# Three tables rewritten: the order, the engines and the PSUM banks of a recorded program of 1187 operations

## The chip, the cores and the metric

The kernel runs on one core of one Trainium2 chip. A core has five instruction queues that run side by side: TensorE (PE, matrix products into PSUM), VectorE (DVE), ScalarE (ACT), GpSimd (POOL) and SyncE (SP), which here only starts DMA transfers. Each engine executes its queue in order. The metric is the device time of one execution in microseconds (us), taken over several runs; beside it stands one execution that was profiled, with the start and end of every instruction.

## The reference

The reference applies two layers, A and B, and then both once more to the result. S = 2048 positions, D = 512 channels, F = 1376, all in bf16:

```python
def A(q, k, v, shift_k, ssm_k, ssm_D):        # q is LayerNorm(x)
    k_shift = sum over t of k_pad[:, t:t+S] * shift_k[:, 3-t]      # 4 taps, along the positions
    kv = k_shift * v
    y = irfft(rfft(kv, 2*S) * rfft(ssm_k, 2*S))[:S]                # causal convolution, 2048 long
    return q * (y + kv * ssm_D)

def B(x, w1, b1, w2, b2):                     # x is LayerNorm(x)
    return gelu(layernorm(x) @ w1 + b1) @ w2 + b2

x = A_q
x = x + A(layernorm(x), k, v, ...);  x = x + B(layernorm(x), ...)
x = x + A(layernorm(x), k, v, ...);  x = x + B(layernorm(x), ...)
```

What A multiplies its q with, the convolution result y + kv * ssm_D, depends on k, v and the filters alone, so both applications share it.

## The kernel before, in words

**Recording and arranging.** The kernel function doesn't emit instructions. It calls `P.op(...)` for each operation, which records the engines that it may run on, what it reads and writes, its PSUM tile and a duration from the writer's own table. Then `arrange()` (line 214) gives each operation its place by three tables of the class `Prog`: `SEQ` is one sequence of all 1187 operation numbers, and an engine's queue is its own operations in that sequence; `ENGS` has a letter for each operation with a choice of engine (a for ACT, v for DVE, p for POOL); `BANKS` gives each PSUM tile its first bank of eight. Operations that follow each other in a bank get a dependence there. `sync()` derives from the queues which semaphore waits are needed, and `emit()` writes the five queues. Data dependences alone limit the order, and every wait is found anew from the tables.

**The convolution, done as a long transform in two matrix stages.** The halves of the time axis are handled one after the other (half 0 first, then half 1). The names are those of the code and of this text, with the lines where the instructions are issued:

- Warm-up: seven matmuls on zeros (L532), so that PE has work before data lands.
- taps: shift_k (4 taps x 512 channels) is transposed on PE (L541) and copied by DVE (L481); POOL makes four diagonal matrices of it (L548).
- ht0, ht1: the filter ssm_k is transposed on PE (L561), a half at a time, and copied out of PSUM by ACT (L480) or DVE (L481); POOL or DVE (L475) adds ssm_D at the first tap.
- h1, h2: the filter's transform. Stage 1 (h1, L578) and stage 2 (h2, L590) are matmuls against tables; each result goes through an evacuation from PSUM by ACT (L480) or DVE (L481).
- spread: half of stage 2's table S2 is built on the chip from a smaller table C, eight steps of 128 x 1024 by ACT (L519) or DVE (L520); the other half of S2 is loaded (tab_s, L470). A part of w1 is later loaded over C, so that load waits for the spread.
- fir0 to fir3 (first half of the positions): k is transposed on PE (L610) and copied, the 4-tap shift is done as matmuls against the diagonals (L635), and DVE multiplies by v (L641). fir4 to fir7 (second half) do the same by pairs (L663, product L672), with k transposed by DMA transposes on SP's queue (L800, "kt").
- x1, x2: the transform of kv, stages 1 and 2, through the same lines L578 and L590. The products of the two spectra are x2_0 and x2_1 on DVE (L475), where half-swapped copies of the filter's spectrum are made by DMAs on SP's queue (L460, ar<-ar). The "sums" (L475, 128x2048) add the two parts of the second half.
- i1, i2: the inverse transform, L695 and L717, again with evacuations by ACT or DVE.

**The two layers, by blocks.** The 16 slices of 128 positions go through A's last step and B in blocks, `BLOCKS` = ((1,1,2,2,2),(2,2,2,2)) slices for the two applications in the first half, and ((4,4),(4,4)) in the second. For each block: q (statistics of x on DVE, L831 and L832; then small steps L836, L838 and the negative mean, L843 on DVE or L846 on POOL; then the normalization, L856 on ACT or L857 on DVE), y (two products on DVE, L475), z (statistics again and a second normalization), a transpose of z (on PE, L908, for the first two blocks; by SP's DMA transpose, L900, for the rest), m1 (44 matmuls, L920, with gelu on ACT, L925) and m2 (matmuls L954, with the addition to x on DVE, L958; the very last slice in three pieces, L943 and L947).

While the blocks of the first half run, PE, DVE and ACT work on the second half's transform in between: h2_1, fir4 to fir7, x1_1, x2_1, the sums and i1_1.

**Loads.** All loads stand in SP's queue apart from three small ones on ACT's. SP executes its queue in order as well: a DMA that has to wait for an engine holds those behind it.

Of the kernel before, what the change touches and what calls it, by code (L numbers as in the profile page):

```python
# [36 lines left out]
class Prog:  # L37
# [7 lines left out]
        0, 46, 8, 45, 35, 2, 6, 3, 5, 36, 12, 9, 1, 10, 11, 25, 4, 44, 217, 7, 56, 197, 15, 50, 16, 57, 14, 13, 47,  # L45
        51, 58, 20, 52, 48, 73, 17, 24, 65, 74, 49, 137, 71, 66, 216, 43, 200, 59, 72, 138, 61, 23, 60, 101, 34, 99,
        102, 198, 62, 26, 63, 212, 30, 135, 37, 100, 38, 53, 390, 18, 39, 103, 22, 432, 27, 41, 105, 19, 104, 108,
        204, 42, 54, 28, 199, 106, 114, 21, 64, 55, 136, 116, 391, 40, 115, 69, 110, 392, 70, 393, 31, 67, 109, 107,
        111, 68, 394, 117, 33, 112, 395, 119, 29, 123, 118, 124, 143, 32, 144, 131, 120, 81, 113, 474, 213, 79, 82,
        125, 80, 126, 127, 132, 433, 434, 75, 128, 435, 76, 121, 133, 476, 122, 77, 304, 475, 78, 129, 134, 528, 91,  # L50
        130, 139, 92, 85, 140, 214, 94, 89, 86, 477, 175, 478, 93, 90, 215, 163, 176, 479, 205, 83, 584, 480, 164, 87,
        84, 145, 88, 187, 165, 171, 188, 96, 177, 167, 95, 172, 168, 149, 97, 296, 150, 146, 179, 98, 183, 170, 180,
        195, 191, 173, 210, 157, 192, 208, 174, 202, 169, 184, 201, 159, 189, 196, 161, 303, 160, 207, 181, 155, 211,
        185, 162, 203, 141, 193, 206, 142, 194, 224, 166, 158, 220, 190, 156, 186, 218, 178, 436, 221, 222, 182, 225,
        582, 230, 219, 223, 232, 481, 231, 228, 484, 530, 233, 226, 583, 229, 227, 151, 437, 147, 295, 152, 148, 234,
        153, 235, 284, 585, 529, 236, 291, 154, 396, 238, 397, 237, 531, 398, 242, 290, 239, 438, 399, 240, 439, 400,
        243, 485, 285, 401, 440, 244, 288, 241, 259, 402, 441, 403, 442, 532, 245, 443, 289, 404, 256, 405, 246, 444,
        533, 445, 424, 260, 209, 410, 422, 425, 586, 286, 446, 261, 423, 587, 406, 447, 294, 418, 257, 250, 407, 388,
        419, 414, 482, 411, 389, 448, 415, 258, 292, 456, 449, 466, 534, 457, 454, 483, 467, 412, 486, 455, 452, 588,
        293, 413, 458, 487, 408, 464, 409, 489, 420, 459, 468, 453, 488, 253, 287, 465, 490, 251, 469, 491, 416, 421,  # L60
        428, 492, 417, 252, 538, 297, 426, 493, 254, 450, 496, 247, 255, 429, 427, 497, 451, 248, 494, 460, 262, 249,
        461, 495, 265, 592, 539, 462, 266, 470, 589, 268, 267, 463, 430, 535, 270, 263, 471, 269, 536, 431, 472, 264,
        298, 537, 272, 540, 518, 541, 271, 504, 519, 543, 502, 505, 542, 590, 506, 503, 593, 512, 507, 544, 591, 510,
        545, 513, 594, 500, 546, 511, 299, 498, 501, 595, 516, 547, 499, 514, 473, 548, 508, 596, 301, 524, 549, 509,
        597, 550, 525, 300, 517, 551, 515, 598, 638, 305, 599, 600, 302, 520, 636, 601, 602, 277, 521, 604, 603, 637,
        312, 307, 313, 526, 639, 309, 605, 640, 522, 641, 306, 554, 308, 642, 273, 568, 646, 527, 552, 274, 569, 572,
        523, 275, 643, 562, 276, 556, 555, 560, 553, 564, 693, 561, 558, 557, 644, 566, 559, 647, 691, 570, 563, 624,
        571, 645, 610, 573, 278, 567, 606, 565, 612, 607, 692, 279, 574, 611, 613, 625, 324, 649, 310, 648, 316, 311,
        694, 280, 695, 575, 317, 283, 608, 696, 620, 609, 576, 621, 281, 325, 614, 697, 320, 577, 615, 322, 321, 282,
        314, 318, 701, 650, 578, 651, 315, 698, 579, 652, 699, 319, 653, 702, 654, 580, 700, 323, 703, 622, 655, 581,  # L70
        628, 623, 704, 656, 326, 706, 618, 657, 327, 705, 658, 338, 707, 746, 708, 334, 339, 709, 659, 328, 616, 626,
        619, 710, 354, 617, 747, 748, 335, 632, 340, 711, 633, 713, 336, 712, 350, 629, 627, 749, 351, 337, 714, 750,
        630, 330, 355, 329, 342, 751, 331, 634, 631, 672, 343, 332, 662, 752, 346, 673, 668, 387, 663, 356, 674, 669,
        385, 678, 347, 384, 670, 344, 386, 664, 675, 717, 665, 333, 719, 679, 660, 720, 666, 661, 341, 729, 671, 718,
        721, 345, 733, 722, 723, 730, 676, 352, 715, 677, 735, 724, 716, 727, 348, 667, 725, 734, 731, 353, 737, 732,
        753, 680, 349, 756, 686, 681, 357, 687, 736, 728, 726, 688, 635, 360, 860, 362, 361, 754, 689, 370, 857, 757,
        368, 371, 755, 758, 682, 759, 369, 761, 683, 363, 760, 762, 801, 372, 763, 764, 862, 358, 373, 803, 765, 364,
        359, 802, 366, 858, 804, 738, 768, 766, 805, 365, 806, 367, 684, 769, 807, 739, 859, 863, 864, 808, 376, 767,
        861, 865, 685, 378, 811, 866, 867, 809, 374, 690, 812, 379, 810, 741, 813, 868, 375, 814, 742, 377, 816, 869,
        782, 875, 774, 815, 872, 783, 772, 817, 876, 878, 818, 776, 873, 819, 870, 775, 770, 879, 773, 743, 820, 771,  # L80
# [914 lines left out]
```

## Time and profile before

| | |
|---|---|
| median of three runs | 236.95 us (236.30 to 237.21) |
| span of the profiled execution | 234.03 us |
| PE busy | 222.7 us, 95% |
| DVE busy | 178.7 us, 76% |
| ACT busy | 164.5 us, 70% |
| POOL busy | 55.5 us, 24% |
| granted TensorE clock | 1.00 throughout |
| DMA | 24.93 MB, mean 107 GB/s |

The span runs from the profiled execution's first instruction to its last. The median of the runs stands 2.92 us above it. An instruction counts as busy while it executes, which for matmuls is modelled; "idle before" is time in which an engine's next instruction waited, and the arrow names what ended that wait. A group of instructions that share a line, an engine, an operation and a shape is one row. The timelines join neighbouring instructions of the same kind, with their count, and give the start, the time that they took together and in brackets the wait ahead of the first.

In the names, ar is the one large SBUF buffer, sm the small one for statistics, ps PSUM, and in_..._dram and tab_... are inputs and tables in DRAM.

### The profile page before, as it was taken

What the parts mean: (1) busy time and instruction counts of PE and PEld (TensorE: products, weight loads), DVE (VectorE), ACT (ScalarE), POOL (GpSimd) and SP (SyncE); (2) the same over time, 40 slices, a digit from 0 to 9 for tenths busy, and PEclk for the clock granted to TensorE, in tenths of its full rate; (3) what the DMA queues carried; (4) which work ended last, traced back from release to release, by engine and by line L of the source; (5) the groups of instructions that cost most, each with busy time, mean ns of one, the idle gap of its engine ahead of it and who ended that gap; (6) DMA issues with size and microseconds to landing.
All of it is one profiled execution on the core that took longest, in us unless ns stands there. A gap on an engine that the chain in (4) does not pass through costs nothing.

```text
span 234.0 us, 6498 instructions
## 1 busy us (share of the span) xinstructions
PE 222.7 (95%) x2743; PEld 147.1 (63%) x2765; DVE 178.7 (76%) x362; ACT 164.5 (70%) x262; POOL 55.5 (24%) x113
## 2 busy tenths in 40 slices
PE   7989887999999999999999999999999999999995
PEld 3878776967868596677966576644444444444454
DVE  0699998999999999999999988781777569410222
ACT  2789999989968688999879986488058216802710
POOL 2270132006403405639303331204011120200000
PEclk9999999999999999999999999999999999999999
DMA  6999489928994360033500313401300130170202
GB/s 185 381 386 305 147 229 274 324 65 150 144 211 126 70 158 3 1 48 72 155 4 3 90 24 68 134 3 22 69 0 3 28 62 0 23 115 0 90 0 92
DMA packets 40106, 24.93 MB, mean 107 GB/s; under 512 B 23591, under 2 KB 33677, under 8 KB 40077
## 3 DMA queue, kind: packets, MB, share of 16 engines
q1 hardware_dynamic: 39778, 24.36, 39.7%
q8 instruction: 22, 0.36, 0.7%
q10 hardware_dynamic: 298, 0.16, 0.4%
q14 instruction: 8, 0.06, 0.1%
HBM read 13.23 MB, written 2.10 MB: 66 GB/s over the span
## 4 chain that ended last, share of the span: by engine, by line
PE 58%; DVE 24%; ACT 10%; issue 2%; POOL 2%; DMA 2%; SPq 0%; DVEq 0%
PE ps L920 23%; PE ps L954 23%; DVE ar L475 13%; ACT ar L480 9%; PE ps L695 4%; DVE sm L831 3%; PE ps L590 2%; DMA ar<-in_A_ssm_k_dram 2%; DVE ar L672 2%; DVE ar L958 2%; DVE ar L641 2%; PE ps L717 1%; POOL sm L836 1%; PE ps L578 1%; PE ps L635 1%
## 5 line engine op out<-in xcount | busy, mean ns | idle before, releaser
L925 ACT ACTIVATE ar<-ps,sm 128x256 bf16<-128x256 f32 (+5 forms) x143 | 65.7, 523 | 33.2 <-PE ps L920 32.9
L920 PE MATMUL ps<-ar 128*128 128x256 bf16 (+5 forms) x569 | 81.9, 297 | 0.4 <-ACT ar L480 0.2
L480 ACT ACTIVATE ar<-ps 128x1024 bf16<-128x1024 f32 (+3 forms) x77 | 71.1, 998 | 11.0 <-PE ps L578 3.4
L954 PE MATMUL ps<-ar 128*128 128x512 bf16 (+1 forms) x323 | 75.9, 379 | 1.5 <-issue 0.6
L920 PEld LDWEIGHTS ps<-ar 128*128 128x128 bf16 (+1 forms) x572 | 52.9, 100 | 27.5 <-ACT ar L480 1.1
L475 DVE TENSOR_TENSOR ar<-ar 128x512 bf16<-128x512 bf16 (+2 forms) x104 | 62.7, 646 | 1.5 <-ACT ar L480 0.8
L954 PEld LDWEIGHTS ps<-ar 128*128 128x128 bf16 (+1 forms) x341 | 32.4, 98 | 35.3 <-ACT ar L925 0.4
L958 DVE TENSOR_TENSOR ar<-ar,ps 128x512 bf16<-128x512 bf16 x31 | 20.8, 680 | 32.9 <-PE ps L954 32.9
L831 DVE BATCH_NORM_STATS2 sm<-ar 128x6 f32<-128x512 bf16 x64 | 42.5, 685 | 0.5
L856 ACT ACTIVATE ar<-ar,sm 128x512 bf16<-128x512 bf16 x39 | 30.6, 813 | 12.9 <-DVE sm L843 8.8
L836 POOL TENSOR_SCALAR sm<-sm 128x2 f32<-128x2 f32 (+2 forms) x22 | 9.9, 449 | 89.0 <-DVE sm L832 88.8
L838 POOL TENSOR_TENSOR sm<-sm 128x2 f32<-128x2 f32 (+2 forms) x26 | 21.7, 834 | 25.1 <-DVE sm L836 23.1
L590 PE MATMUL ps<-ar 128*128 128x64 bf16 x512 | 18.4, 193 | 1.5 <-DVE ar L481 0.7
L578 PE MATMUL ps<-ar 128*64 128x128 bf16 x512 | 17.9, 221 | 1.8 <-ACT ar L480 1.2
L590 PEld LDWEIGHTS ps<-ar 128*128 128x128 bf16 x512 | 16.8, 98 | 3.6 <-DVE ar L481 1.3
L578 PEld LDWEIGHTS ps<-ar 128*64 128x64 bf16 x512 | 14.9, 110 | 4.8 <-ACT ar L480 1.9
L481 DVE CAST ar<-ps 128x1024 bf16<-128x1024 f32 x12 | 14.6, 1218 | 1.2 <-PE ps L578 0.9
L846 POOL TENSOR_SCALAR sm<-sm 128x1 f32<-128x1 f32 x34 | 15.1, 460 | 1.6
L695 PE MATMUL ps<-ar 64*128 64x64 bf16 (+1 forms) x384 | 12.4, 203 | 1.0 <-DVE ar L475 0.9
L695 PEld LDWEIGHTS ps<-ar 64*128 64x128 bf16 (+1 forms) x384 | 11.8, 113 | 2.2 <-DVE ar L475 1.0
L857 DVE TENSOR_SCALAR ar<-ar,sm 128x512 bf16<-128x512 bf16 x25 | 10.3, 415 | 2.7 <-POOL sm L846 2.5
L788 DVE SCALAR_TENSOR_TENSOR ar<-ar,sm,ps 128x512 bf16<-128x512 bf16 x16 | 11.1, 740 | 0.3 <-PE ps L590 0.3
(45 smaller groups left out, 93.5 us busy)
## 6 DMA issues: line engine op xcount, KB each, us to landing
ar<-ar SPq DMA_DIRECT2D x16, 256.0 KB, 4.0
ar<-tab_s SPq DMA_DIRECT2D x9, 256.0 KB, 6.3
ar<-in_A_ssm_k_dram SPq DMA_DIRECT2D x8, 256.0 KB, 5.9
ar<-in_A_q_dram SPq DMA_DIRECT2D x8, 256.0 KB, 4.4
ar<-in_A_v_dram SPq DMA_DIRECT2D x8, 256.0 KB, 5.0
out_dram<-ar SPq DMA_DIRECT2D x7, 256.0 KB, 2.5
ar<-in_B_w_dram SPq DMA_DIRECT2D x4, 344.0 KB, 5.2
ar<-in_B_w_dram SPq DMA_DIRECT2D x5, 256.0 KB, 5.2
```

The costliest lines, as they stand in the source:

```text
L475: return P.op(eng, lambda e: e.tensor_tensor(o, a, b, op), dur, reads=[a, b] + list(more), writes=[o])
L480: return e.activation(dst, src(), AF.Copy)
L578: r = e.matmul(Q(tl, 64 * ri, 64, i * 128, [1, 128]), w, m, start=True, stop=True)
L590: r = e.matmul(Q(tl, 0, 128, i // 8 * 512 + i % 8 * 4, [32, 16], [1, 4]), w, m, start=True, stop=True)
L695: r = e.matmul(Q(tl, 0, 128, i, *([32, 16], [1, 4]) if split else ([1, 128],)), w, m, start=n == 0, stop=n == 1)
L831: P.op(DVE, lambda e, sj=sj, x=x: e.bn_stats(sj, x), 600.0, reads=[x], writes=[sj])
L838: P.op(POOL, lambda e: e.tensor_tensor(r, v, hf, ALU.pow), 420.0 + 149.0 * n, reads=[v, hf], writes=[r])
L856: return e.activation(o, x, AF.Identity, bias=u, scale=r)
L920: r = e.matmul(Q(tl, 0, rows, 0, [1, w]), a, m, start=dk == 0, stop=dk == 3)
L925: P.op(ACT, lambda e, dst=dst, tl=tl, rows=rows, bias=bias, w=w: e.activation(dst, Q(tl, 0, rows, 0, [1, w]), AF.Gelu_apprx_tanh, bias=bia ...
L954: r = e.matmul(Q(tl, 0, 128, 0, [1, 512]), ins[fc][0], ins[fc][1], start=fc == 0, stop=fc == 10)
L958: P.op(DVE, lambda e, x=x, tl=tl: e.tensor_tensor(x, x, Q(tl, 0, 128, 0, [1, 512]), ALU.add), 604.0, reads=[x], writes=[x], tile=tl)
```

## The change

Only the three tables are rewritten. No operation is added, removed or changed in what it reads, writes and computes. 46 operations change their engine (ACT has 263 operations instead of 266, DVE 364 instead of 362, POOL 92 instead of 91), 441 operations have another PSUM bank, and the sequence is another one throughout. The matmuls are the same.

```diff
 class Prog:
     SEQ = (
-        0, 46, 8, 45, 35, 2, 6, 3, 5, 36, 12, 9, 1, 10, 11, 25, 4, 44, 217, 7, 56, 197, 15, 50, 16, 57, 14, 13, 47,
-        51, 58, 20, 52, 48, 73, 17, 24, 65, 74, 49, 137, 71, 66, 216, 43, 200, 59, 72, 138, 61, 23, 60, 101, 34, 99,
...
+        8, 35, 0, 25, 36, 1, 37, 6, 5, 2, 9, 197, 11, 38, 3, 56, 57, 50, 10, 51, 12, 47, 48, 390, 432, 43, 58, 73, 4,
+        52, 74, 71, 65, 7, 391, 392, 66, 433, 13, 27, 49, 61, 72, 62, 31, 15, 59, 216, 45, 60, 101, 102, 99, 63, 100,
...
     ENGS = (
-            "pvavvvvvavpvpapapaaavaaaaavaavaavavvvppvvvaavvaaavaavvaaaaaaaaavaaaaavaaaavaaaaaaapppvaaaaaaaaaaaaaaaaaa"
...
+            "pvvavvvavvpapvpapaaavaaaaavaavaavavvappppaaavvaaavavvvaaaaaaaaavaaaaavaaaavaaaaaaappvpaaaaaaaaaaaaaaaaaa"
...
     BANKS = (
-            "26624320240260660466027405640260464422140204626240406006442460424046462022442640460444626002206020640220"
...
+            "20073220440262240466027610646260464026341344006200442066402460624023624022442660460444626004262606002224"
...
```

The rows below show the queues as the tables give them, one row for neighbouring instructions of the same kind, without times.

The first place is the head of the kernel, on ACT and DVE, as far as the filter's transposes and the first results of stage 1. 128x8x16x8 is a copy of ht0, 128x1024 an evacuation of a transform stage, 128x8x128 a copy of a transposed k, 128x64x16 a step of the spread. On ACT (a minus stands for the row before, a plus for the row now):

```order
 L470 DMA ar<-tab_small 128x464
+L460 DMA ar<-in_A_shift_k_dram 4x512
 L460 DMA ar<-in_A_ssm_D_dram 1x512
 L494 ACT_TABLE_LOAD
-L460 DMA ar<-in_A_shift_k_dram 4x512
-L480 ACTIVATE ar<-ps 128x8x16x8
+L480 ACTIVATE ar<-ps 128x8x16x8 x2
 L480 ACTIVATE ar<-ps 128x1024 x4
 L480 ACTIVATE ar<-ps 128x8x128
```

The shift_k load moved ahead of the ssm_D load, and a second ht0 copy stands at ACT's head. On DVE before:

```order
L481 COPY ar<-ps 128x8x16x8 x2
L481 CAST ar<-ps 128x1024
L481 COPY ar<-ps 128x8x128
L520 TENSOR_SCALAR ar<-ar,sm 128x64x16 x2
L481 COPY ar<-ps 128x4x4
L831 BN_STATS sm<-ar 128x6 x2
L481 COPY ar<-ps 128x8x128
L520 TENSOR_SCALAR ar<-ar,sm 128x64x16
```

And on DVE now:

```order
L481 COPY ar<-ps 128x4x4
L481 COPY ar<-ps 128x8x16x8
L831 BN_STATS sm<-ar 128x6 x2
L832 BN_AGGR sm<-sm 128x2
L836 TENSOR_SCALAR sm<-sm 128x1
L481 CAST ar<-ps 128x1024
L832 BN_AGGR sm<-sm 128x2
L520 TENSOR_SCALAR ar<-ar,sm 128x64x16 x2
```

The taps' copy (128x4x4) went to the head, one ht0 copy left, and two statistics of q stand ahead of the first cast. On PE the transposes of the taps moved in the same way, from behind h1_0's first matmuls to right behind the warm-up.

The second place is SP's queue where the tables of stage 2 (tab_s) and the second half of the filter (in_A_ssm_k_dram) are loaded. Before:

```order
L470 DMA ar<-tab_small 128x256
L460 DMA ar<-in_A_q_dram 128x1024
L460 DMA ar<-in_B_b_dram 128x10x1
L460 DMA ar<-in_A_ssm_k_dram 128x1024
L470 DMA ar<-tab_s 128x1024 x3
L460 DMA ar<-in_B_w_dram 128x1376
L460 DMA ar<-in_A_q_dram 128x1024
L470 DMA ar<-tab_s 128x1024
L460 DMA ar<-in_A_ssm_k_dram 128x1024
```

Now:

```order
L460 DMA ar<-in_A_ssm_k_dram 128x1024
L470 DMA ar<-tab_s 128x1024
L460 DMA ar<-in_B_w_dram 128x1376
L470 DMA ar<-tab_s 128x1024 x3
L460 DMA ar<-in_A_ssm_k_dram 128x1024
L470 DMA ar<-tab_s 128x1024 x3
L460 DMA ar<-in_A_ssm_k_dram 128x1024
```

The load of the part of w1 (128x1376), which waits for the spread's last reading of C, now stands ahead of eight loads of the tables and the filter instead of two. Farther ahead in the same queue, the first load of q went from the tenth place to the fifth, with k's other three loads and a table behind it; and the last of the eight DMA transposes of k (L800) went behind two transposes of z (L900) and four half-swaps (L460, 64x8x256).

The third place is DVE's queue around the long run of sums that i1_1 reads (128x32x64 is a sum or a product of x2_1, L958 the addition of m2). Before:

```order
L475 TENSOR_TENSOR ar<-ar 128x32x64 x2
L832 BN_AGGR sm<-sm 128x2
L475 TENSOR_TENSOR ar<-ar 128x32x64 x2
L958 TENSOR_TENSOR ar<-ar,ps 128x512
L475 TENSOR_TENSOR ar<-ar 128x32x64 x11
L958 TENSOR_TENSOR ar<-ar,ps 128x512
```

Now:

```order
L475 TENSOR_TENSOR ar<-ar 128x32x64 x3
L832 BN_AGGR sm<-sm 128x2
L475 TENSOR_TENSOR ar<-ar 128x32x64
L958 TENSOR_TENSOR ar<-ar,ps 128x512
L475 TENSOR_TENSOR ar<-ar 128x32x64 x12
L475 TENSOR_TENSOR ar<-ar 128x512
L958 TENSOR_TENSOR ar<-ar,ps 128x512
```

The run behind that L958 is of twelve instead of eleven, so one more sum stands behind the addition. Other additions of m2 stand farther forward in DVE's queue, the one of operation 635 at place 173 of DVE's operations instead of 190.

In the chain of z of the first block, the negative mean is computed on POOL (L846) instead of DVE (L843).

8 lines of the change are left out of this document (4 added, 4 removed), and 106 rows, old and new, of the table SEQ.

## The prediction

> **What bounds the kernel now.** I read the busy time by stretch first. The columns are the stretch's length, and then the busy time of PE, of its weight loads (PEld), of DVE, ACT and POOL, each with its instructions; then the granted clock, the DMA share and the rate.
>
> ```profile
> 5.70:41.30 35.60, 30.84 (x772) 27.05 (x770) 31.75 (x52) 32.70 (x35) 9.69 (x24) 1.00 0.89 285
> 41.30:56.40 15.10, 14.32 (x243) 11.87 (x244) 14.71 (x33) 13.89 (x18) 2.23 (x6) 1.00 0.69 181
> 56.40:121.40 65.00, 64.08 (x917) 48.19 (x927) 64.11 (x109) 57.05 (x114) 25.25 (x40) 1.00 0.44 95
> 121.40:227.30 105.90, 104.99 (x764) 55.10 (x775) 66.28 (x168) 59.58 (x97) 16.95 (x34) 1.00 0.18 41
> ```
>
> From 56.4 on PE is busy for all but 0.92 of 65.00 and all but 0.91 of 105.90 us, at the full clock. The diff changes no matmul, so little is to be had behind 56.4. Ahead of it PE idles 4.76 us of 35.60 and 0.78 of 15.10. What holds PE there is shown by the chain of work that ended last (start, duration, what):
>
> ```profile
> 34.14 1.85 ACT ar L480 x2
> ...
> 39.97 1.30 DVE ar L475 x2
> 41.27 0.05 issue
> 41.32 7.39 PE ps L695 x128
> 48.73 6.59 ACT ar L480 x8
> 55.37 0.41 PE ps L908 x4
> ...
> 56.46 0.84 PE ps L920 x12
> ```
>
> The inverse transform i1_0 (L695) begins at 41.32, when the last spectrum product x2_0 (L475 on DVE) is done; these products in turn read ACT's PSUM evacuations (L480). Then come evacuations of i1_0, the transposes of z0 (L908) and at 56.46 the first matmul of m1 (L920). By the two orders the same 55 PE operations stand ahead of i1_0 before and after, and the same 75 ahead of the first m1. So the forecast is: the shift of i1_0, plus the change of the chain to 56.46, plus what the later stretches lose or win.
>
> Next I asked for what ACT, DVE and POOL themselves waited in the first 42 us (total, times, longest):
>
> ```profile
> POOL ar L548 <- DVE ar L481: 3.1, 1, 3.1
> ACT ar L480 <- PE ps L561: 2.6, 1, 2.6
> ACT ar L480 <- PE ps L578: 2.3, 3, 1.4
> DVE ar L481 <- PE ps L561: 6.9, 2, 6.6
> ```
>
> And for ACT's own timeline (start, duration, idle ahead in brackets):
>
> ```profile
> 5.70 1.02 ACT L480 ACTIVATE ar<-ps 128x1024 bf16<-128x1024 bf16 x1 [2.63 <-PE ps L561]
> 8.14 4.69 ACT L480 ACTIVATE ar<-ps 128x1024 bf16<-128x1024 f32 x5 [1.42 <-PE ps L578]
> 16.41 1.94 ACT L480 ACTIVATE ar<-ps 128x1024 bf16<-128x1024 f32 x2 [0.73 <-PE ps L578]
> 18.23 1.15 ACT L519 ACTIVATE ar<-ar,sm 128x1024 bf16<-128x1024 bf16 x1
> 30.37 17.65 ACT L480 ACTIVATE ar<-ps 128x1024 bf16<-128x1024 f32 x19 [0.17 <-PE ps L590]
> ```
>
> From 5.70 on ACT is nearly full: 32.70 of 35.60, idle 2.90, half of it the gap of 1.42. DVE idles 35.60 - 31.75 = 3.85, of which 0.85 lies ahead of its first copy at 6.55 (the wait of 6.6 above); 3.00 remain. The last evacuation that x2_0 needs is the ninth of the run at 30.37 (17.65 / 19 = 0.93 each), so it ends at 38.73; four products stand behind it on DVE.
>
> **The change part by part.** All of it is order, engine and bank. The durations are:
>
> ```profile
> L480 ACT ACTIVATE ar<-ps 128x1024 bf16<-128x1024 f32 x27 | 25.6, 1033 | 2.9 <-PE ps L578 2.3 <-PE ps L590 0.6
> L481 DVE CAST ar<-ps 128x1024 bf16<-128x1024 f32 x8 | 9.8, 1220 | 0.9 <-PE ps L578 0.6 <-PE ps L590 0.3
> L480 ACT ACTIVATE ar<-ps 128x1024 bf16<-128x1024 bf16 x5 | 5.2, 1037 | 2.6 <-PE ps L561 2.6
> L481 DVE COPY ar<-ps 128x1024 bf16<-128x1024 bf16 x7 | 4.8, 683 | 7.6 <-PE ps L561 6.9 <-PE ps L610 0.7
> L856 ACT ACTIVATE ar<-ar,sm 128x512 bf16<-128x512 bf16 x1 | 0.8, 812 | 0.0
> L857 DVE TENSOR_SCALAR ar<-ar,sm 128x512 bf16<-128x512 bf16 x25 | 10.3, 415 | 2.7 <-POOL sm L846 2.5
> ```
>
> *ACT up to x2_0's last evacuation.* It takes four evacuations more (one of ht0, one transpose of fir3, one of x1_0, one of h1_1), gives up two (of ht0 and ht1) and one L856, and swaps two steps of the spread for two others: 4 x 1.035 - 2 x 1.037 - 0.81 = +1.26. Before, it worked 38.73 - 5.70 - 2.90 = 30.13 there; now 31.4. With all 2.90 of idle kept it ends at 40.0; with none, at 37.1. Two gaps have a reason to go. The ht0 copy that it takes is ready when the gap of 1.42 begins. And the taps (below) bring FIR work forward, behind which the gap of 0.73 stood. That leaves 0.75 idle and an end at 37.85. One product instead of four now follows the last evacuation, 0.65 by the chain (1.30 for two). So i1_0 begins between 38.5 and 40.7, that is 0.6 to 2.8 earlier, by ACT alone.
>
> *DVE up to the same point.* It gives up two bf16 copies and one cast (1.37 + 1.22), and takes two copies and one L857 (1.37 + 0.41): 0.8 less. With its 3.00 of idle kept and 0.5 lost at the head (next), it gains 0.3; with all idle gone, 3.8. Both engines have to be there. I take 1.7, the middle of ACT's range, since ACT is the fuller of the two.
>
> *Heads of the queues.* The taps' transposes go from behind h1_0 to right behind the warm-up matmuls, and the shift_k load ahead of ssm_D. POOL's diagonals (L548) waited 3.1 for the taps' copy, so FIR can begin about 1 us earlier: that is the 0.73 counted above. On DVE two BN_STATS of q now stand ahead of the first cast. They wait for a q load that moves from the tenth place of SP's load queue to the fifth; if it lands late, DVE stands with a cast behind it. From the start of a load to its landing:
>
> ```profile
> L460 SPq DMA_DIRECT2D ar<-in_A_k_dram x4: 432/432/435, 2.1 to 3.5; - x4
> ...
> DMA to landing us min/median/max: 5.5/5.8/6.1
> ```
>
> The fifth load is issued at about 2.6, so it lands at 8.1 to 8.7, where the first cast began at 8.59 before. Two BN_STATS then push that cast by 1.3, against one copy of 0.68 that DVE no longer does: from nothing to 0.6, taken as 0.5. The k loads behind it land a place later, half a microsecond; FIR reads them only after the taps: nothing, unless the taps are so early that k is then last.
>
> *z0's chain.* One mean step goes from DVE (L843) to POOL (L846), 0.27 for 0.14:
>
> ```profile
> 54.46 0.14 DVE L843 SCALAR_TENSOR_TENSOR sm<-sm 128x1 f32<-128x1 f32 x1
> 55.84 0.27 POOL L846 TENSOR_SCALAR sm<-sm 128x1 f32<-128x1 f32 x1
> ```
>
> That is 0.13; with the other engine's start I take +0.2, between 0 and the 1.3 of a rival below.
>
> *56.4 to the end.* The m2 additions (L958) stand earlier in DVE's queue, and DVE executes in order. What DVE waited for them over the whole run, the end of the spectrum sums, and what they feed:
>
> ```profile
> DVE ar L958 <- PE ps L954: 32.9, 12, 7.4
> ...
> 108.41 12.58 DVE L475 TENSOR_TENSOR ar<-ar 128x2048 bf16<-128x2048 bf16 x11
> ...
> 121.44 2.57 PE L695 MATMUL ps<-ar 64*128 64x64 bf16 x128
> ```
>
> The first matmul of i1_1 (121.44) needs all sixteen sums, done at 120.99: 0.45 spare. DVE's work ahead of the last sum falls by the 0.8 above and by one L857 (0.41), 1.2 in all; if its idle in the front falls with PE's, it keeps up with PE 1.7 earlier. I put zero here, with 0 to +3 as bounds. The sixth to eighth transposes of A_k and the FIR that reads them:
>
> ```profile
> L800 SPq DMA_TRANSPOSE ar<-in_A_k_dram x8: 1188/1268/2345, 49.3 to 61.2; - x8
> ...
> L663 PE MATMUL ps<-ar x176: 172/201/225, 69.4 to 78.0; 32*128 32x128 bf16 x80, 32*128 32x32 bf16 x32, 32*128 32x64 bf16 x32, 32*128 32x96 bf16 x32
> ```
>
> The eighth goes behind two transposes of z2 and four half-swaps, which wait for DVE; its FIR goes behind m1 of block 2, 5.7 us of PE work. I cost this at nothing; the FIR at 69.4 was covered by other matmuls, and without them the transpose would cost its own issue, 1.2 to 2.3. At the tail the order of matmuls and stores is nearly the same: nothing. The PSUM banks move for 441 operations; no wait for a bank stands out above, and I give them nothing.
>
> *Sum.* -1.7 + 0.2 = -1.5, on a profiled span of 234.03: 232.5. The median of the runs stands 2.9 above that span (236.95 - 234.03); with it 235.4.
>
> **The rivals.** *The front gains as worked out:* 235.4, with its own bounds. If all of ACT's 2.9 and the three products were saved it would be 3.4 (233.5); if only 0.6 at i1_0 and +0.2 at z0, 236.5.
>
> *DVE loses it in order (slower).* If the earlier L958 make DVE wait between 56 and 121, the sums come late and i1_1 with them. It can lose 0.45 (spare) + 1.2 (less work) + 0.9 (the front's idle, 1.7 - 0.8) = 2.55 before i1_1 is later than it was; from there the end is slower than before. One wait of the length that L958 showed elsewhere, 7.4, gives 4.85 on the end: 241.8; two thirds of such a wait, 4.9, give 2.35: 239.3. For it: DVE busy 64.11 of 65.00. Against: m2's matmuls are moved forward with their additions, and the window's whole idle time on DVE was 0.89.
>
> *Loads hold the front.* In SP's queue a w1 load now waits for the spread's last reading of the C table, and eight loads stand behind it, tables of h2_0 among them. The spread's last step on ACT ended at 19.4 (18.23 + 1.15). These loads were
>
> ```profile
> 16.96 3.36 SPq L470 DMA_DIRECT2D ar<-tab_s  x3
> ...
> 21.31 0.43 SPq L470 DMA_DIRECT2D ar<-tab_s  x1
> ```
>
> so the last table was issued at 21.3. Eight at 0.48 from 19.4 end at 23.2, 1.9 later, and land at 29. If h2_0 is ahead by then, it loses the 1.9: 237.3. Against: h2_0 reads half its table from the spread first.
>
> *POOL's steps are held beside DVE.* In z0's chain three steps run on POOL. A POOL step of 0.2 to 0.3 took this long beside three DVE products:
>
> ```profile
> 90.35 3.34 POOL L836 TENSOR_SCALAR sm<-sm 128x2 f32<-128x2 f32 x1 [8.07 <-DVE sm L832]
> ...
> 90.16 3.48 DVE L475 TENSOR_TENSOR ar<-ar 128x2048 bf16<-128x2048 bf16 x3
> ...
> L475 DVE TENSOR_TENSOR ar<-ar x104: 392/425/1237, 32.5 to 197.7; 128x512 bf16<-128x512 bf16 x64, 128x2048 bf16<-128x2048 bf16 x24, 128x1024 bf16<-128x1024 bf16 x16
> ```
>
> If each step waits out one product of 0.42, that is 1.3 in place of 0.2: 236.5. [...] Against it here: the step at 55.84 took its 0.27 while DVE was busy too.
>
> *Nothing on the path changes:* PE's idle in the front is put elsewhere, 236.95.
>
> **How the numbers follow.** A measurement of this kernel tells about 0.5% from no change, 1.2 us: faster is under 235.8, slower over 238.1. The front's gain 0.49; DVE's loss 0.26; late loads 0.13; POOL held 0.07; nothing 0.05. The last three lie within 0.5%. So faster 0.49, same 0.25, slower 0.26. The range goes from 233.5, the whole of ACT's idle gained, to 239.3, two thirds of a long L958 wait; beyond it lie half of DVE's rival (0.13) and little below.
>
> **What would show it.** In the changed kernel's profile i1_0 (L695) begins near 39.6 and the first L920 near 55; ACT has no gap of 1.4 at 6.7 to 8.1; L548 begins about 1 us earlier or more; DVE between 55 and 120 idles no more than 1 to 2 us; the first L695 of i1_1 stands near 120. The forecast is wrong if i1_0 stays behind 41, if a weight load of h2_0 names a DMA as what it waited for, or if L695 near 120 waits for DVE.

## The result

The changed kernel takes 238.97 us (median of four runs, 238.48 to 239.90) against 236.62 for the kernel before (four runs, 235.60 to 237.21): the ratio is estimated as 1.0119, with a 95% interval from 1.0081 to 1.0158. By the medians it is 2.35 us slower, a quotient of 1.0099; the ratios given below are estimates of the same kind, and need not be the quotients of the medians. The profiled spans say the same: 236.73 against 234.03.

The busy times by stretch, of the changed kernel (columns as in the prediction):

```profile
5.70:41.30 35.60, 30.87 (x783) 27.84 (x781) 31.15 (x49) 33.80 (x37) 10.99 (x28) 1.00 0.93 291
41.30:56.40 15.10, 14.26 (x244) 11.54 (x242) 14.75 (x32) 13.70 (x17) 4.03 (x13) 1.00 0.44 140
56.40:121.40 65.00, 61.49 (x903) 45.99 (x904) 60.59 (x105) 55.48 (x110) 20.19 (x35) 1.00 0.50 101
121.40:227.30 105.90, 105.90 (x780) 55.24 (x779) 70.20 (x176) 60.32 (x97) 16.97 (x35) 1.00 0.17 41
```

PE's idle time in the front is as it was (4.73 for 4.76). Between 56.4 and 121.4 it is 3.51 for 0.92: that is the loss. Behind 121.4 PE is full. The chain of work of the changed kernel, front part:

```profile
30.57 4.99 DMA ar<-ar
35.56 0.02 issue
35.58 0.87 DVE ar L475 x2
...
40.54 7.39 PE ps L695 x128
...
54.53 0.40 PE ps L908 x4
...
55.86 0.45 PE ps L920 x8
```

The front does gain: i1_0 begins at 40.54 for 41.32, the transposes of z0 at 54.53 for 55.37, m1 at about 0.7 earlier. But the chain goes through a DMA, a half-swap that lands at 35.56, where the prediction had ACT.

PE's own timeline shows where the middle lost it (idle ahead in brackets):

```profile
75.00 1.12 PE L663 MATMUL ps<-ar 32*128 32x128 bf16 x88 [0.83 <-ACT ar L856]
...
95.27 1.53 PE L578 MATMUL ps<-ar 128*64 128x128 bf16 x48 [1.05 <-ACT ar L925]
...
110.28 0.64 PE L590 MATMUL ps<-ar 128*128 128x64 bf16 x16 [1.54 <-ACT ar L480]
```

Measured from start to start, which leaves the modelled ends out, these cost 1.0, 1.2 and 1.7 us. Behind each stands another engine. POOL, then DVE, then ACT around the last two:

```profile
57.21 0.50 POOL L846 TENSOR_SCALAR sm<-sm 128x1 f32<-128x1 f32 x2
...
90.97 2.67 POOL L846 TENSOR_SCALAR sm<-sm 128x1 f32<-128x1 f32 x2
...
103.47 3.39 POOL L846 TENSOR_SCALAR sm<-sm 128x1 f32<-128x1 f32 x2
```

```profile
57.10 1.40 DVE L788 SCALAR_TENSOR_TENSOR ar<-ar,sm,ps 128x512 bf16<-128x512 bf16 x2
...
90.83 2.68 DVE L475 TENSOR_TENSOR ar<-ar 128x512 bf16<-128x512 bf16 x3
...
103.22 3.50 DVE L475 TENSOR_TENSOR ar<-ar 128x2048 bf16<-128x2048 bf16 x3
...
110.26 14.14 DVE L475 TENSOR_TENSOR ar<-ar 128x2048 bf16<-128x2048 bf16 x13 [1.68 <-ACT ar L480]
```

```profile
93.68 0.81 ACT L856 ACTIVATE ar<-ar,sm 128x512 bf16<-128x512 bf16 x1 [1.37 <-POOL sm L846]
...
106.89 1.52 ACT L856 ACTIVATE ar<-ar,sm 128x512 bf16<-128x512 bf16 x2 [1.72 <-POOL sm L846]
```

Such a pair of POOL steps takes 0.50 beside DVE's L788, which has one of its two large inputs in PSUM, and 2.67 and 3.39 beside DVE's products and sums L475, which have both in SBUF (the row at 90.83 is one product and two sums); it ends when they do (106.86 beside 106.72, 93.64 beside 93.51). No experiment takes the products and sums away from the step; that they hold it is read from these coincidences, and what in them does so is not shown. ACT's normalization L856 waits for it, the gelus and PSUM evacuations behind L856 wait in ACT's queue, and PE and then DVE itself wait for those. The trace of before has the steps of q6 (94.58) and of z6 (101.86) too, and the L856 that wait for them:

```profile
94.58 1.16 POOL L846 TENSOR_SCALAR sm<-sm 128x1 f32<-128x1 f32 x2
...
101.86 1.05 POOL L846 TENSOR_SCALAR sm<-sm 128x1 f32<-128x1 f32 x2
```

```profile
95.77 0.81 ACT L856 ACTIVATE ar<-ar,sm 128x512 bf16<-128x512 bf16 x1 [0.16 <-POOL sm L846]
...
103.68 1.57 ACT L856 ACTIVATE ar<-ar,sm 128x512 bf16<-128x512 bf16 x2
```

There q6's chain was held as well, one step earlier (3.34 at 90.35, in the prediction), and its mean was ready later than now, at 95.74 for 93.64. PE did not wait there: four evacuations of x1_1, with gelus among them, stood ahead of that L856 in ACT's queue. A pair of q7 took 4.54 at 108.54, and its L856 came at 118.25 only. The wait at 75 has a different cause, which the experiments show.

### The profile page after: what moved, and what is told of

The parts are those of the page before. It is cut to its first block, busy times and chain, and to the rows that moved or that the text cites. A ratio compares the mean times of both kernels' runs of the same rounds, so it can differ in the third digit from the quotient of the medians.

```text
span 236.7 us, 6529 instructions
## 1 busy us (share of the span) xinstructions
PE 224.0 (95%) x2765; PEld 146.7 (62%) x2765; DVE 179.7 (76%) x364; ACT 164.6 (70%) x259; POOL 53.2 (22%) x117
## 4 chain that ended last, share of the span: by engine, by line
PE 77%; DVE 7%; DMA 5%; ACT 4%; SPq 2%; POOL 2%; issue 1%
PE ps L920 32%; PE ps L954 29%; PE ps L695 5%; DMA ar<-in_A_k_dram 3%; DVE ar L475 3%; SPq L460 2%; ACT ar L480 2%; DMA ar<-ar 2%; PE ps L590 2%; PE ps L578 2%; DVE ar L481 2%; PE ps L635 2%; POOL sm L846 2%; DVE sm L831 2%; PE ps L717 1%
## 5 line engine op out<-in xcount | busy, mean ns | idle before, releaser
L925 ACT ACTIVATE ar<-ps,sm 128x256 bf16<-128x256 f32 (+5 forms) x143 | 66.4, 526 | 43.2 <-PE ps L920 42.9
L920 PE MATMUL ps<-ar 128*128 128x256 bf16 (+5 forms) x572 | 80.9, 297 | 0.0
L480 ACT ACTIVATE ar<-ps 128x1024 bf16<-128x1024 f32 (+3 forms) x79 | 72.3, 1002 | 8.9 <-PE ps L561 2.4
L954 PE MATMUL ps<-ar 128*128 128x512 bf16 (+1 forms) x341 | 78.3, 379 | 0.1
L475 DVE TENSOR_TENSOR ar<-ar 128x512 bf16<-128x512 bf16 (+2 forms) x104 | 63.2, 641 | 3.9 <-ACT ar L480 1.9
L958 DVE TENSOR_TENSOR ar<-ar,ps 128x512 bf16<-128x512 bf16 x31 | 21.0, 682 | 20.0 <-PE ps L954 19.7
L856 ACT ACTIVATE ar<-ar,sm 128x512 bf16<-128x512 bf16 x34 | 26.7, 808 | 7.4 <-POOL sm L846 5.0
L838 POOL TENSOR_TENSOR sm<-sm 128x2 f32<-128x2 f32 (+2 forms) x26 | 21.6, 830 | 44.7 <-DVE sm L836 43.0
L836 POOL TENSOR_SCALAR sm<-sm 128x2 f32<-128x2 f32 (+2 forms) x19 | 4.9, 257 | 86.8 <-DVE sm L832 85.7
L590 PE MATMUL ps<-ar 128*128 128x64 bf16 x512 | 18.4, 193 | 1.8 <-ACT ar L480 1.7
L578 PE MATMUL ps<-ar 128*64 128x128 bf16 x512 | 17.6, 221 | 2.4 <-ACT ar L480 1.3
L590 PEld LDWEIGHTS ps<-ar 128*128 128x128 bf16 x512 | 16.8, 98 | 3.7 <-ACT ar L480 2.5
L578 PEld LDWEIGHTS ps<-ar 128*64 128x64 bf16 x512 | 14.8, 110 | 4.8 <-ACT ar L480 2.3
L846 POOL TENSOR_SCALAR sm<-sm 128x1 f32<-128x1 f32 x39 | 15.3, 408 | 1.8
L857 DVE TENSOR_SCALAR ar<-ar,sm 128x512 bf16<-128x512 bf16 x30 | 11.7, 410 | 5.0 <-POOL sm L846 4.7
L695 PEld LDWEIGHTS ps<-ar 64*128 64x128 bf16 (+1 forms) x384 | 11.7, 113 | 2.8 <-DVE ar L475 1.9
L695 PE MATMUL ps<-ar 64*128 64x64 bf16 (+1 forms) x384 | 12.2, 203 | 1.3 <-DVE ar L475 1.3
L481 DVE CAST ar<-ps 128x1024 bf16<-128x1024 f32 x10 | 12.0, 1216 | 0.2 <-PE ps L590 0.2
L788 DVE SCALAR_TENSOR_TENSOR ar<-ar,sm,ps 128x512 bf16<-128x512 bf16 x16 | 10.9, 733 | 0.0
```

The costliest lines, as they stand in the source:

```text
L475: return P.op(eng, lambda e: e.tensor_tensor(o, a, b, op), dur, reads=[a, b] + list(more), writes=[o])
L480: return e.activation(dst, src(), AF.Copy)
L578: r = e.matmul(Q(tl, 64 * ri, 64, i * 128, [1, 128]), w, m, start=True, stop=True)
L590: r = e.matmul(Q(tl, 0, 128, i // 8 * 512 + i % 8 * 4, [32, 16], [1, 4]), w, m, start=True, stop=True)
L695: r = e.matmul(Q(tl, 0, 128, i, *([32, 16], [1, 4]) if split else ([1, 128],)), w, m, start=n == 0, stop=n == 1)
L838: P.op(POOL, lambda e: e.tensor_tensor(r, v, hf, ALU.pow), 420.0 + 149.0 * n, reads=[v, hf], writes=[r])
```

## The experiments

All kernels have the same operations, and all are compared with the kernel before, timed beside them (median 235.97 to 236.24 there; 236.62 beside the changed kernel), so ratios rather than times are to be compared. The changed kernel itself has its four runs alone, and its interval is wide. Only tables were edited; the diffs are of the engines' queues that the tables give.

### The front and the rest exchanged

The cut is the first m1 matmul of each sequence.

```diff
 e1: SEQ  = changed[: first m1] + [i for i in before if not in it];  engines and banks accordingly
 e2: SEQ  = before[: first m1] + [i for i in changed if not in it];  engines and banks accordingly
```

> The changed kernel's tables up to its first m1 matmul (303 operations, with their engines and banks), then the kernel before's order, engines and banks for the rest. Theory A (the loss lies behind the first m1, in three stalls of PE that the new order of the middle makes: 1.0 at 74, 1.2 at 94, 1.7 at 108): this kernel keeps only the front's gain of 0.4 to 0.6 us and ends at 236.0 to 236.3, ratio 0.997 to 0.999. Theory B (the new front moves POOL, DVE and ACT against each other, and the stalls behind it are its consequence): this kernel shows them too, ratio over 1.005.

> The reverse: the kernel before's tables up to its first m1 (308 operations), then the changed order, engines and banks. Theory A: the three stalls stay and the front's gain is gone, 2.3 + 0.5 over the kernel before: 239.3 to 239.7, ratio 1.011 to 1.013. Theory B: no more than 0.5 us over the kernel before, ratio under 1.003.

Measured: e1 235.60, ratio 0.9977 (0.9955 to 0.9999); e2 238.88, ratio 1.0112 (1.0092 to 1.0133). The stretch from 56.4 to 121.4 of e1, with the changed front ahead of it:

```profile
56.40:121.40 65.00, 64.97 (x966) 48.33 (x965) 64.03 (x110) 56.28 (x113) 21.25 (x37) 1.00 0.41 91
```

PE idles 0.03 there. So the changed front is good for 0.5 us, and does not cause what follows: theory A. In e2 the eighth transpose of A_k belongs to the first part and so keeps its old place; its wait is absent, the wait of 1.7 at 108 is there (1.54 in the row, as in the changed kernel), the one at 94 isn't, and a wait of 1.3 for a transpose of z3 at 83 is new. POOL's pair of q6 is held for 2.67 there too, but PE, held at 83, comes to that place 1.8 later. So the waits are those of the changed middle, though not each of them in every company.

### The eighth transpose of A_k

```diff
 SP's queue, e3:
-L800 DMA_TRANSPOSE ar<-in_A_k_dram 128x4x128 x3
+L800 DMA_TRANSPOSE ar<-in_A_k_dram 128x4x128 x4
 L460 DMA ar<-in_A_v_dram 128x1024 x2
 L900 DMA_TRANSPOSE ar<-ar 128x4x128 x2
 L460 DMA ar<-in_A_v_dram 128x1024
-L460 DMA ar<-ar 64x8x256 x4
-L800 DMA_TRANSPOSE ar<-in_A_k_dram 128x4x128
-L460 DMA ar<-ar 64x8x256 x4
+L460 DMA ar<-ar 64x8x256 x8
```

> The changed kernel with one DMA moved on SP's queue: the eighth transpose of A_k stands behind the seventh again, ahead of z2's transposes and the half-swaps. Theory A: it lands near 68 instead of 74.9, fir5's matmuls (L663) no longer wait at 73 to 75, and the end is 1.0 earlier, 238.0, if nothing behind takes it back. Rival: the profile names ACT's L856 for that wait; if it is right the wait stays and the time is 239.0. Third: PE gains 1.0 at 75 and loses it again at 94 and 108, where it waits for a chain through POOL that does not start earlier: 239.0 with the wait at 75 gone.

Measured: 242.40, ratio 1.0246 (1.0212 to 1.0280), 3.4 slower than the changed kernel, which no theory had. The transpose landed at 67.4 and fir5 no longer waited for it; but z2's two transposes, now behind it, landed at 71.3 and 71.8 instead of 67.8 and 68.3, and m1 of block 2 stood for them:

```profile
71.84 6.64 PE L920 MATMUL ps<-ar 128*128 128x256 bf16 x44 [2.34 <-DMA ar<-ar]
...
71.60:76.00 4.40, 4.16 (x23) 3.32 (x24) 4.26 (x14) 2.00 (x5) 2.44 (x7) 0.61 1.13 300
```

The second row is PE's stretch behind that wait: the granted clock is 0.61 there, and a matmul of m1 takes 421 ns in the median for 272 where the clock is full. The 44 matmuls took 6.64 us for 4.98 in the changed kernel (68.32), so 1.7 of PE's time went that way, besides the 2.5 of the wait. So the DMA queue between 62 and 72 is the scarce thing: a place behind z2 and the swaps costs fir5 1.0, and one ahead of them costs m1, which reads z2, the 2.5.

### Two means moved from POOL to DVE

```diff
 DVE's queue, e4 (and the two L846 pairs gone from POOL's):
 L831 BN_STATS sm<-ar 128x6
 L475 TENSOR_TENSOR ar<-ar 128x512
+L843 SCALAR_TENSOR_TENSOR sm<-sm 128x2
 L475 TENSOR_TENSOR ar<-ar 128x32x64 x2
...
 L857 TENSOR_SCALAR ar<-ar,sm 128x512
 L831 BN_STATS sm<-ar 128x6
+L843 SCALAR_TENSOR_TENSOR sm<-sm 128x2
 L475 TENSOR_TENSOR ar<-ar 128x32x64 x3
```

> The changed kernel with two negative-mean steps (of q6 and z6) on DVE (L843, 0.15) instead of POOL (L846, which took 2.67 and 3.39 beside DVE's products), the second one place later in DVE's queue. Theory A: what held PE at 94 and 108 was POOL's step, for which ACT's normalization L856 waited with PSUM evacuations queued behind it; the waits of L856 go, and 2.0 to 2.9 us with them: 236.1 to 237.0. Rival: DVE itself is the bound there and PE waits for its products in any case: less than 0.5 us gained. Second rival: the neighbouring POOL steps (L836, L838) are held in its place: half of it, 237.5 to 238.

Measured: 237.06, ratio 1.0029 (1.0008 to 1.0050): 1.9 us less than the changed kernel by the medians, 0.9% by the ratios. PE's rows at the two places, and the one that stays:

```profile
76.17 1.12 PE L663 MATMUL ps<-ar 32*128 32x128 bf16 x88 [1.16 <-ACT ar L925]
...
94.74 1.98 PE L578 MATMUL ps<-ar 128*64 128x128 bf16 x64
...
108.35 0.63 PE L590 MATMUL ps<-ar 128*128 128x64 bf16 x16
```

Both waits are gone, and the steps take 0.15 and 0.16 on DVE. 2.9 us of waits removed gave 1.9: in this profile fir5 waited 1.3 by starts, 0.3 more, and the first m2 matmul 0.4 for a load of w2 (see below). One mean alone, that of z6, with that of q6 left on POOL:

```diff
 DVE's queue, e11:
 L857 TENSOR_SCALAR ar<-ar,sm 128x512
 L831 BN_STATS sm<-ar 128x6
+L843 SCALAR_TENSOR_TENSOR sm<-sm 128x2
 L475 TENSOR_TENSOR ar<-ar 128x32x64 x3
```

> The changed kernel with one mean alone (z6) on DVE; that of q6 stays on POOL. If the two held steps count one after the other, PE's wait at 108 (1.7) goes and that at 94 (1.2) stays: 237.2 to 237.8, and the step of z6 takes 0.15. If the earlier one is the cause of the later one (POOL, late by the first, is late for the second), the gain is under 0.7: 238.3 or more.

Measured: 238.12, ratio 1.0078 (1.0051 to 1.0104), so 0.9 to 1.0 less than the changed kernel, which is half of what both gave and less than expected. Its interval lies above e4's, but overlaps the changed kernel's. In its profile the wait at 108 is gone and that at 94 stays:

```profile
97.11 1.53 PE L578 MATMUL ps<-ar 128*64 128x128 bf16 x48 [1.06 <-ACT ar L925]
```

So the wait at 108 comes from z6's own step, not from the wait at 94; q6's step alone was not moved, and the time stays between the two expectations. (This profile lost another 1.3 at 8 to 12 us, to the clock; the last section has the row.)

The third way to take the wait away leaves POOL's steps alone:

```diff
 ACT's queue, e7:
 L856 ACTIVATE ar<-ar,sm 128x512
-L480 ACTIVATE ar<-ps 128x2x16x32
+L480 ACTIVATE ar<-ps 128x2x16x32 x3
 L856 ACTIVATE ar<-ar,sm 128x512 x2
-L480 ACTIVATE ar<-ps 128x2x16x32 x4
+L480 ACTIVATE ar<-ps 128x2x16x32 x2
```

> The changed kernel with POOL's steps where they are, but with two evacuations of x2_1 (L480) moved ahead of the two normalizations L856 of z6 in ACT's queue (and the two transposes of z6 behind them on SP). If PE waited at 108 because its evacuations stood behind an L856 that waited for POOL, the step on POOL is still held for 3.4 us, and the PE wait of 1.7 is gone nevertheless: 1.2 to 1.7 gained, 237.3 to 237.8. If the POOL step itself is what the path needs (z6 to m1 of block 6), the gain is under 0.5.

Measured: 240.40, ratio 1.0192 (1.0164 to 1.0220), so slower still, which neither expectation had. Of e7, POOL and then PE:

```profile
105.69 3.39 POOL L846 TENSOR_SCALAR sm<-sm 128x1 f32<-128x1 f32 x2
```

```profile
110.81 0.63 PE L590 MATMUL ps<-ar 128*128 128x64 bf16 x16
...
112.88 0.61 PE L920 MATMUL ps<-ar 128*128 128x256 bf16 x4 [0.57 <-ACT ar L480]
113.80 0.61 PE L920 MATMUL ps<-ar 128*128 128x256 bf16 x4 [0.30 <-ACT ar L480]
115.04 1.92 PE L920 MATMUL ps<-ar 128*128 128x256 bf16 x16 [0.63 <-DMA ar<-ar]
```

POOL's step is held for 3.39 as before; the evacuations go ahead of it and L590 at 110.81 no longer waits. The time comes back at once: the next m1 matmuls wait 0.7, 0.5 and 0.8 by starts, at last for the transposes of z6, whose L856 went back. So both are needed by PE, the evacuations and the mean, and the cure is the step that isn't held. (This profile also has the w2 wait of 1.7 described below, so its total says little. What makes the six runs slower than the changed kernel's is not shown.)

### The front: q's load, and what bounds i1_0

```diff
 SP's queue, e5 (and on DVE the two BN_STATS of q a few places later):
 L460 DMA ar<-in_A_ssm_k_dram 128x1024 x3
-L460 DMA ar<-in_A_k_dram 128x1024
-L460 DMA ar<-in_A_q_dram 128x1024
-L460 DMA ar<-in_A_k_dram 128x1024 x3
+L460 DMA ar<-in_A_k_dram 128x1024 x4
 L470 DMA ar<-tab_s 128x1024
 L460 DMA ar<-in_A_ssm_k_dram 128x1024
+L460 DMA ar<-in_A_q_dram 128x1024
```

> The changed kernel with the first q load back at the tenth place of SP's loads and the two statistics that read it a few places later in DVE's queue. Theory: in the fifth place it pushes the landing of k's last load from 9.6 to 11.4, for which the transposes of k (L610) wait at 10 to 11.5; now they start at about 10 and PE is 1.0 to 1.6 earlier there, and the end with it: 237.4 to 238.0. Rival: i1_0 is held by the half-swaps (the fourth took 5.0 from 30.6 on, and DVE's products waited 0.8 for it), so the front gives it back: 238.5 to 239.

Measured: 239.84, ratio 1.0181 (1.0150 to 1.0212): no gain, rather 0.6% more than the changed kernel, and no trace shows why, since the profiled run (238.83) was the fastest of the six. In the changed kernel PE waited for k, in e5 it doesn't:

```profile
PE ps L610 <- DMA ar<-in_A_k_dram: 1.6, 1, 1.6
```

```profile
DVE ar L475 <- DMA ar<-ar: 0.6, 1, 0.6
...
PE ps L610 <- ACT ar L480: 0.2, 1, 0.2
```

The 1.6 are gone at 10 us, and z0's transposes begin at 54.38 for 54.53. So the front gave most of them back, to the half-swaps that DVE's products need. In the fifteen profiles of the two kernels and the variants the start of i1_0 follows the landing of the fourth half-swap. It landed between 35.1 and 36.8 in eight of them, and i1_0 began 4.98 to 5.05 later in each, which is eight products; it landed at 33.8 to 34.2 in the other seven, when DVE still had a cast to do, and i1_0 began 5.7 to 5.8 later. In the second group the eighth half-swap takes over (in all but e12). The chain of e1 shows that:

```profile
33.23 1.76 SPq L460
34.99 0.04 issue
35.03 0.59 SPq L460
35.63 0.04 issue
35.67 4.73 DMA ar<-ar
40.40 0.02 issue
40.42 2.07 DVE ar L475 x4
...
44.18 3.78 PE ps L695 x64
...
54.56 0.40 PE ps L908 x4
```

The step of 1.76 is the issue of a load of 0.2 KB (the end of b1) that the change put between the sixth half-swap and the seventh. Two kernels take only that away, one with the changed front and the old rest (e13, beside e1), one with all corrections (e12, beside e10 below):

```diff
 SP's queue, e13 against e1 (e12 against e10 alike):
-L460 DMA ar<-ar 64x8x256 x6
 L460 DMA ar<-in_B_b_dram 96x1
-L460 DMA ar<-ar 64x8x256 x2
+L460 DMA ar<-ar 64x8x256 x8
```

> The changed front with the rest of the kernel before, and the same small load ahead of the half-swaps. Swaps theory: the eighth swap lands about 39.5 instead of 40.4, the 0.9 that DVE waited for it goes, z0's transposes start near 53.8 instead of 54.56, and the end is 0.5 to 0.9 earlier: 234.7 to 235.1, ratio 0.993 to 0.996. ACT theory: as without, 235.6, ratio 0.998.

> The kernel with the four corrections, and the small load of b1's last part (0.2 KB) ahead of the eight half-swaps on SP's queue instead of between the sixth and the seventh. If the front is bound by the landing of the half-swaps (in twelve profiles i1_0 began 5.0 to 5.8 behind the landing of the fourth), the seventh and eighth are issued 0.65 or more earlier, DVE's last products wait less, and z0's transposes and the end come 0.5 to 1.0 earlier than without: 234.2 to 234.7. If ACT's evacuations bind it, no difference: 235.2.

Measured: e13 234.62, ratio 0.9935 (0.9914 to 0.9956), against 0.9977 without; e12 235.16, ratio 0.9964 (0.9943 to 0.9986), the same as without and as its rival had it. In e12's profile the eighth half-swap landed at 38.31 (40.82 without) and DVE runs through its fourteen products:

```profile
34.90 8.51 DVE L475 TENSOR_TENSOR ar<-ar 128x1024 bf16<-128x1024 bf16 x14
```

z0's transposes begin at 53.90, the earliest of all profiles. In e13's profile, of the slowest of its six runs, the fourth half-swap landed late, at 36.13, and z0 began at 55.12 in spite of an eighth that landed at 39.31. So the traces show that the swaps bound the start of i1_0 and of z0. What freeing the last two is worth is shown by e13's time alone; e12's time does not show it. Why the fourth half-swap lands 3.8 us after its issue in some profiles (e3, e6, e9) and 4.9 to 5.0 in others (the changed kernel, e4, e7, e11), whose queues are the same up to there, stays open.

### The other loads, and the corrections together

```diff
 SP's queue, e6 (with the two means of e4), against the changed kernel:
 L900 DMA_TRANSPOSE ar<-ar 128x4x128 x2
+L800 DMA_TRANSPOSE ar<-in_A_k_dram 128x4x128
 L460 DMA ar<-in_A_v_dram 128x1024
-L460 DMA ar<-ar 64x8x256 x4
-L800 DMA_TRANSPOSE ar<-in_A_k_dram 128x4x128
-L460 DMA ar<-ar 64x8x256 x4
+L460 DMA ar<-ar 64x8x256 x8
```

> The changed kernel with the two means on DVE, and the eighth transpose of A_k right behind z2's two transposes on SP's queue, ahead of the half-swaps. Theory: it lands near 71, fir5 no longer waits (1.0 to 1.3 at 74), z2 is not delayed as it was by the transpose ahead of it, and the time is that of the means alone less about 1.2: 235.8. Rival: the half-swaps, now 1.3 to 2 later, hold DVE's products p2 or the next transposes of z, and it stays at 237.

Measured: 235.89, ratio 1.0005 (0.9987 to 1.0023). That is 0.2% under the means alone, and the two intervals overlap, so what the transpose gives is shown by the trace alone: it landed at 70.4, and fir5 no longer waits. Another wait shows ahead of it:

```profile
64.10 1.67 PE L954 MATMUL ps<-ar 128*128 128x512 bf16 x7 [1.29 <-ACT ar L856]
...
75.45 1.13 PE L663 MATMUL ps<-ar 32*128 32x128 bf16 x88
```

The first m2 matmul at 64.10 needs a w2 load that the change put between transposes of A_k; it landed at 63.80, just ahead of it, though the row names ACT.

```diff
 SP's queue, e9 against the changed kernel:
-L460 DMA ar<-in_B_w_dram 128x2x512
+L460 DMA ar<-in_B_w_dram 128x2x512 x2
 L800 DMA_TRANSPOSE ar<-in_A_k_dram 128x4x128
 L460 DMA ar<-in_B_w_dram 128x2x512
 L460 DMA ar<-in_A_v_dram 128x1024
-L800 DMA_TRANSPOSE ar<-in_A_k_dram 128x4x128 x3
-L460 DMA ar<-in_B_w_dram 128x2x512
-L800 DMA_TRANSPOSE ar<-in_A_k_dram 128x4x128 x3
+L800 DMA_TRANSPOSE ar<-in_A_k_dram 128x4x128 x6
```

> The changed kernel with one load moved on SP's queue: a fifth of w2 (256 KB) stands with the other w2 loads again, ahead of the transposes of A_k. In its changed place it landed at 61.5 in the changed kernel's profile and at 62.8 to 64.4 in three of its variants, where the first m2 matmul (due at 62.5) waited 0.3 to 1.7 for it. Theory: that is a fourth cause, which strikes by chance in some runs; with the load early the first m2 starts at 62.5 in each, 0.3 to 1.0 off the median: 238.0 to 238.7. Rival: m2 is held by the gelu of its block in any case: 239.0.

Measured: 239.92, ratio 1.0145 (1.0113 to 1.0178), no gain. m2 starts at 62.81 without a wait, but m1 of block 2 then waits longer for z2's transposes, so the time is given back on the same queue:

```profile
69.62 4.98 PE L920 MATMUL ps<-ar 128*128 128x256 bf16 x44 [0.98 <-DMA ar<-ar]
```

The w2 load is late in some executions (it landed at 63.80 in e6's profile and at 61.5 in the changed kernel's) and costs nothing of its own that shows in the time. Then the corrections together:

```diff
 e8:  the changed kernel + the queues of e6 + the queues of e5
 e10: e8 + the queue of e9
```

> The changed kernel with the three corrections: q load late, two means on DVE, the eighth transpose of A_k right behind z2's. If the three causes add up, 1.9 + 1.2 + 1.0 to 1.6 off 239.0: 234.3 to 234.9, ratio to the kernel before 0.992 to 0.996, faster than both. If they hide one another: 236 or more.

> The kernel with the three corrections, and the w2 load early. By the theory its profiled wait of 1.5 at 62.9 to 64.2 goes: 234.2 to 235.0, ratio 0.990 to 0.995. If that wait was covered elsewhere: 235.4, ratio 0.997.

Measured: e8 235.43, ratio 0.9969 (0.9951 to 0.9988); e10 235.17, ratio 0.9964 (0.9940 to 0.9989). Both are faster than the kernel before by 0.3 to 0.4% and than the changed one by 1.5%, though less than expected; against e6 the q and w2 loads are within the intervals. The fastest of the study is e13, the changed front with the old rest and the small load out of the swaps' way: 0.65% under the kernel before.

## Why the prediction was wrong

It forecast 235.4 and faster; it was slower. Of its three signs of being wrong none came: i1_0 began before 41, no L590 waited for a DMA, and L695 near 120 did not wait for DVE. But DVE idled 4.41 us between 55 and 120, where it had allowed 1 to 2. Step by step:

**i1_0, -1.7: half of it, and by another cause.** ACT did lose its gap of 1.42 (0.37 is left): it is busy for 33.80 of 35.60, for 32.70 before. But it idles 1.80 and not the 0.75 of the sum, since the gap of 0.73 stayed (0.62) and one of 0.76 for k's transposes came. The last evacuation that the products need ended at 38.52 for 38.73, not at 37.85. And it wasn't ACT that held i1_0: in both kernels the product that reads this evacuation began 1.2 to 1.3 after its end. The step that failed is the reading of the chain. The row of before that I took for ACT's hold on DVE is this one:

```profile
36.35 6.11 DVE L475 TENSOR_TENSOR ar<-ar 128x1024 bf16<-128x1024 bf16 x10 [0.82 <-ACT ar L480]
```

The evacuation that this product reads had ended at 35.07, long done; another input, the fourth half-swap, landed at 36.27 in the same trace. After the change the same wait reads `<-DMA ar<-ar`, at 35.58. The half-swap came 0.71 earlier and i1_0 0.78 earlier: DMA, eight products, i1_0, both times; it is the eighth of these products that i1_0 waits for, and not, as the prediction has it, the last, since six more follow on DVE. That i1_0 came earlier at all was luck as far as the argument goes.

**q's load: costed at 0.5 and at nothing for k.** In the changed kernel's profile q landed at 9.42, 2.1 us behind the load ahead of it and not 0.65, as the k loads follow one another; k's last load landed at 11.40 for 9.62, and PE waited 1.6. (In the variants with the same place q landed between 7.5 and 9.1, and PE waited 0.6 to 1.4 by starts, in e11 not at all.) So FIR did not begin 1 us earlier: POOL's diagonals did, at 9.14 for 12.22, but the first L635 came at 14.55 for 13.38. The size was wrong by about three, and by e5's trace it mattered little, since the half-swaps covered it.

**z0's chain, +0.2.** From i1_0 to z0's transposes 13.99 us passed, and 14.05 before: nothing. The rival that POOL's steps are held there did not happen: they took 0.28, 0.55 and 0.27.

**56.4 to the end, zero: the step that turned the sign.** It was bounded by 0 to +3. The three new waits are 3.9 by starts; with the front's 0.76 and 0.4 that came back in small pieces elsewhere, that leaves the 2.7 of the spans. Moving the two POOL steps (e4) took two of the three waits and 1.9 us away. The mechanism that I priced for it, an addition L958 that waits in DVE's queue, was not it: DVE waited 1.2 for L958 between 44 and 128, for 0.5 before. The sums did come late and i1_1 with them (its first matmul at 124.22 for 121.44), but because ACT's evacuations stood behind an L856 that waited for POOL. POOL held beside DVE was among the rivals, with a chance of 0.07, at z0 alone and for 1.3. The row that speaks for it was quoted (3.34 us at 90.35), and I did not ask where else in the changed queues a POOL step that PE needs falls beside a run of products. The chain needs two conditions, the held step and an L856 with work behind it that PE is about to need: one of q6's normalizations was moved to ACT (operation 698, on DVE before) with two gelus behind it, and z6's two stand ahead of evacuations which were due.

Not every run of products holds a POOL step in the changed kernel's trace: a pair of L846 took 0.50 beside L788, which takes one input from PSUM, and 3.39 beside three L475 of 128x2048, but an L838 at 72.78, with two L475 of 128x512 beside it (72.91 and 73.32), took 0.71, as the one at 61.53 beside L788 did (0.72). The rival priced each held step at one product of 0.42; before the change, the one POOL instruction of 3.34 at 90.35 stood through three of DVE's (3.48).

**The eighth transpose, cost at nothing.** It cost 1.0 at 75. I argued that the FIR at 69.4 was covered by other matmuls and now stands behind m1 of block 2. It did go back, to 75.00 for 69.39, but the transpose's landing went back farther, to 74.91 for 66.15, and PE, which takes its queue in order, stood until then. e3 shows that the old place would now cost more, e6 that from a place between them it lands in time for fir5.

**Late loads of the tables.** That rival did not happen: w1's load waited until 20.2 (19.4 by the working), the last table was issued by 24.8, and no L590 waited for a DMA.

## What to carry to other kernels

Where the releaser that a row names had long been done, look up the other inputs of the waiting instruction, DMAs above all, before a forecast is built on it. For a new order of instructions, walk each queue in which a step on POOL or a DMA stands ahead of PSUM evacuations or transposes that PE needs, and ask what DVE runs at that moment: here the two pairs took 2.67 and 3.39 on POOL where DVE did them in 0.15 and 0.16, and PE waited 1.2 and 1.7 behind them. A load that is moved forward or back has to be priced by its neighbours' landing times on the queue, in both directions (m1 of block 2 waited 2.34 for z2 in e3, and 0.98 in e9).

## What the runs showed that I had not expected

In two profiles the granted clock of PE was lower behind a short wait. In e3 a wait of 2.34 us was followed by a granted clock of 0.61 over 4.4 us, in e11 one of 1.60 at 7.4 by this:

```profile
8.00:12.00 4.00, 4.00 (x85) 3.73 (x83) 3.04 (x6) 2.32 (x3) 2.44 (x6) 0.61 1.03 396
```

In e11 it was 0.93 in the stretch ahead of this one (5.7 to 8); in e3 it was 1.00 from 64 to 71.6 and from 76 to 80. PE's matmuls took 1.7 us more in e3's profile (6.64 for 4.98) and 1.3 in e11's (the 80 matmuls L578 at 8.27: 3.75 for the 2.50 of the changed kernel). The length of the wait alone does not decide it. In e5 and e9 L590 waited 1.7 in all for ACT, as in the changed kernel, where 1.54 of it is one wait, and no slice of their pages has a lower clock; and after the wait of 1.62 at 11.49 in the changed kernel, whose profile has no record of the clock, sixteen transposes of k took 1.05 for 1.07 before. What does decide it is not shown.
